# Where the absolute sums over three weight matrices are made: rows of w_sp in z1, wo in the first spatial chunk

## The chip, the core and the metric

The kernel runs on one core of one Trainium2 chip. Five engines, each with its own queue in order, work beside each other: TensorE (PE), VectorE (DVE), ScalarE (ACT), GpSimd (POOL) and SyncE (SP); SP and ACT issue the DMAs. The metric is the device time of one execution in microseconds, the median of several runs.

## What is computed

Two blocks on the same input x (2048 rows, 1024 columns, bf16), mixed by a gate:

```python
x = A_x
g = sigmoid((x * gate_w).sum(-1, keepdims=True))
# A: 32 heads of 32; each row attends to 8 rows, itself and those 2, 4, .. 14 above it
qkv = x @ wqkv; logits = q . k[s - 2w] * 32 ** -0.5; a = (softmax(logits) . v[s - 2w]) @ wo
# B: gMLP
z = gelu(x @ w_in)                       # 3584 columns: z1 the first 1792, z2 the others
z2 = layernorm(z2)                       # over its 1792 columns
gg = einsum('ts,sf->tf', w_sp, z2) + b_sp[:, None]     # w_sp is 2048 x 2048
b = (z1 * gg) @ w_out
return g * a + (1 - g) * b
```

## The kernel before

Nearly all arithmetic is TensorE's, in stages one after the other:

- **z2, first part** (to 37 us of the trace): 128-row tiles of x times 512-column pieces of w_in, gelu on ScalarE (line 308) into the array `z2`.
- **q, k, v** (lines 623 and 643, to 197 us). Rows go to DRAM and come back in another order; the attention itself is VectorE's (lines 349 to 399), eight head groups from here to the end of the spatial chunks, with one exp on ScalarE per group (line 379).
- **z2, second part** (line 303, 198 to 283 us): 14 tiles of 512 columns, then for each of 16 row tiles one of 512 and one of 257 columns (256 and the gate's). ScalarE makes the gelu of each, copies the gate's column (line 312) and, after each pair, sums the squares of the row tile (line 756). VectorE normalizes four row tiles at a time.
- **z1** (line 829, 283 to 380 us): 14 column tiles f, each with four products of 8 matmuls over 512 rows; gelu on ScalarE (line 832) into a slot of `z1s_slots`, from which a DMA stores it to `z1_d` (line 835). The last tiles stay on chip in `z1c_slots` in part.
- **spatial chunks 0 and 1** (`g_chunk`, line 857, 380 to about 482 us): for 512 rows t each, 14 groups of 16 matmuls of z2 by a transposed quarter of w_sp. Each group adds to a PSUM bank that ScalarE has seeded with b_sp (line 787), five groups ahead; ScalarE copies the result out (line 861) and VectorE multiplies it with z1 (line 864).
- **the other 1024 rows** (`seven_products`, line 925): seven products in place of eight, with sums and differences of operands, in fp16 where they are sums. So that they fit, rows of w_sp (and w_out and wo later) are multiplied by powers of two, which are taken from their sums of absolute values.
- **the mix with w_out and wo** (lines 1053 and 1142, to the end).

The sums of absolute values are the subject. Each is one ScalarE instruction over 128 x 2048 elements with an accumulated output, on a block that a DMA has loaded for it:

- *rows of w_sp*, 8 blocks of 128 rows (lines 745 to 748), in z2's second part, with three slots and one junk output in the region EF; they give `row`, from which `row_powers` (lines 799 to 812, VectorE) makes `up` and `down`.
- *w_out* 7 and *wo* 4 blocks (lines 769 to 777), in z1, with two slots in the region CD; they give `w_l1` and `wo_l1`, whose largest values are made powers of two by `whole_power` in three steps.

In chunk 0 the same rows of w_sp are loaded again by DMAs from ScalarE's queue (`natural`, line 872), multiplied by `up` (`scale_rows`: rows 1, 3, 5 on VectorE, line 886; the others on ScalarE, line 890), stored to `wsp_d` (lines 888 and 891) and read back transposed for `seven_products` (line 491, SP). The transposed quarter of w_sp for chunk 1 is loaded by SP at the same time, in four pieces (line 491 too); `scaled_biases` sends the scaled b_sp through DRAM (`bsp_d`, lines 879 and 882), and a pair of attention groups is stored to `o_d` (line 410).

The order is written by hand. A counter of TensorE's columns, `beat`, gives a planned time; `beat.at(t, fn)` puts an instruction into its engine's queue as soon as the matmuls issued so far reach t:

```python
def at(self, t, fn):
    heapq.heappush(self.later, (t, self.n, fn))
def run(self, cols):
    self.now += cols * BEAT          # BEAT = 1 / 2360 us
    self.flush(self.now)
```

VectorE's attention steps are interleaved by an estimate of when VectorE is free. What an engine waits for is set by data and by slots alone, except that every DMA takes one of eight completion counters in turn, over both issuing queues: it isn't issued before the DMA eight places ahead of it has landed.

PSUM has eight banks of 128 x 512 fp32; all stages take theirs from one pool. The names in the profile leave numbers out, so that `z1_d` and `z2_d` are both `z_d`, `w_l1` is `w_l`.

Of the kernel before, what the change touches and what calls it, by code (L numbers as in the profile page):

```python
# [47 lines left out]
CD_OFF = A_OFF + 22016  # L48
EF_OFF = CD_OFF + 19456
# [8 lines left out]
def kernel(  # L58
# [13 lines left out]
    nc = tc.nc  # L72
# [10 lines left out]
    def reg(off, n):  # L83
        return arena[:, off:off + n]
# [32 lines left out]
    row = sm.tile([P, 8], F32, name="row")  # L117
# [6 lines left out]
    w_l1 = sm.tile([P, 7], F32, name="w_l1")  # L124
    v_l1 = s1[:, 0:NF]
    u_l1 = sm.tile([P, NF], F32, name="u_l1")
    top = sm.tile([P, 1], F32, name="top")
# [3 lines left out]
    wo_l1 = sm.tile([P, 4], F32, name="wo_l1")  # L131
# [49 lines left out]
    w1_slots = [reg(EF_OFF + r * 4096, 4096).rearrange("p (k c) -> p k c", k=KT) for r in range(2)]  # L181
    z1s_slots = [reg(EF_OFF + 8192 + r * 2048, 2048).rearrange("p (c t) -> p c t", c=4) for r in range(4)]
    row_slots = [reg(EF_OFF + 10240 + r * 2048, 2048) for r in range(3)]
    row_out = reg(EF_OFF + 8192, 2048)
    wsp_slots = [reg(CD_OFF, 8192).rearrange("p (i a t) -> p i a t", i=16, a=4),
# [10 lines left out]
    nat_slots = [reg(X_OFF + r * S, S) for r in range(8)]  # L196
    look_slots = [reg(CD_OFF + 8192 + r * 2048, 2048) for r in range(2)]
    look_out = reg(CD_OFF + 12288, 2048)
# [32 lines left out]
    wsp_v = B_w_sp.rearrange("(a t) s -> a t s", t=P)  # L231
    wo_v = A_wo.rearrange("(g h d) n -> g h d n", g=NG, h=HG, d=DH)
    sync = nc.sync
# [38 lines left out]
    beat = Beat()  # L272
# [471 lines left out]
    sync.dma_start(b_row[:], bass.AP(tensor=B_b_sp.tensor, offset=B_b_sp.offset + 1024, ap=[[P, 8], [1, P]]))  # L744
    for r in range(8):
        beat.at(beat.now + 1.0 + (1.5 * r if r < 3 else 4.0 * r), lambda r=r: sync.dma_start(row_slots[r % 3], wsp_v[8 + r]))
        beat.at(beat.now + 8.0 + 4.0 * r, lambda r=r: nc.scalar.activation(row_out, row_slots[r % 3], ACT.Abs,  # L747
                                                                           accum_out=row[:, r:r + 1]))
    for i in range(2, 16):
# [17 lines left out]
    wout_v = B_w_out.rearrange("(f p) n -> p f n", p=P)  # L767
    wo_rows = A_wo.rearrange("(k p) n -> p k n", p=P)
    for k in range(11):
        slot = look_slots[k % 2]  # L770
        src = wout_v[:, 2 * k:2 * k + 2, :] if k < 7 else wo_rows[:, 2 * k - 14:2 * k - 12, :]
        total = w_l1[:, k:k + 1] if k < 7 else wo_l1[:, k - 7:k - 6]
        beat.at(beat.now + 2.0 + 7.0 * k, lambda src=src, slot=slot: sync.dma_start(
            slot.rearrange("p (f n) -> p f n", f=2), src))
        beat.at(beat.now + 13.0 + 7.0 * k, lambda total=total, slot=slot: nc.scalar.activation(
            look_out, slot, ACT.Abs, accum_out=total))

    for g in range(NG):
        beat.at(beat.now + 6.0 + 10.0 * g, lambda g=g: turn_wo(g))
    w_steps = whole_power(w_up, omg[:])  # L780
    beat.at(beat.now + 72.0, lambda: (nc.vector.tensor_reduce(top[:], w_l1[:], AX.X, ALU.max), next(w_steps)))

# [30 lines left out]

    beat.at(beat.now + 50.0, row_powers)

    for f in range(NF):
        ch = f // 4
        w1 = w1_slots[ch % 2]
        if f % 4 == 0 and ch in (1, 2):
            load_w1(ch + 1)  # L820
        z1s = z1s_slots[f % 4]
        if f == 4:
# [434 lines left out]
    t0 = beat.now  # L1257
    for r in range(8):
        beat.at(t0 + 6.0 + 3.4 * r, lambda r=r: natural(r))
        beat.at(t0 + 20.0 + 4.0 * r, lambda r=r: scale_rows(r))  # L1260
    for aa in range(4):
        beat.at(t0 + 1.0 + 7.0 * aa, lambda aa=aa: load_wsp(1, aa))
        beat.at(t0 + 50.0 + 2.5 * aa, lambda aa=aa: load_wsp(2, aa))
        beat.at(t0 + 61.0 + 2.5 * aa, lambda aa=aa: load_wsp(3, aa))
# [66 lines left out]
```

## Time and profile before

| | us |
|---|---|
| median of 3 runs | 705.11 (704.88 to 706.19) |
| the profiled execution, its own time | 706.95 |
| its span in the profile | 704.8 |
| TensorE busy | 684.7 |
| VectorE busy | 562.4 |
| ScalarE busy | 416.0 |

The profile gives, for one execution, busy times by engine, the span in 40 slices with the granted TensorE clock and DMA, the chain of work that ended last, and instructions grouped by source line. More views of the trace list who waited for whom, and instructions in order of time: start, duration, engine, line, output and input, and in brackets how long the engine was idle before it and what ended that. In the views of stretches each engine's busy time stands with its instructions in brackets. SPq and ACTq are DMA issues; L747 is line 747.

### The profile page before, as it was taken

How to read it: one execution, taken by the hardware profiler on the slowest of the kernel's cores; microseconds unless marked ns; L12 is line 12 of the kernel's file. 1: busy time of each engine (PE TensorE's matmuls, PEld its weight loads, DVE VectorE, ACT ScalarE, POOL GpSimd, SP SyncE). 2: the span in 40 equal slices, each digit the busy share in tenths (PEclk: the TensorE clock that was granted, in tenths of full speed). 3: DMA queues.
4: the chain of work that ended last, by engine and by line, in shares of the span. 5: the costliest groups of instructions: out<-in, count | busy, mean ns of one | idle time of the engine just before them, and what ended most of it. 6: DMA issues, size and time to landing. Idle time of an engine off the chain costs nothing.

```text
span 704.8 us, 9004 instructions
## 1 busy us (share of the span) xinstructions
PE 684.7 (97%) x3327; PEld 356.2 (51%) x3327; DVE 562.4 (80%) x692; ACT 416.0 (59%) x744; POOL 12.9 (2%) x45
## 2 busy tenths in 40 slices
PE   9999999999996879999999999998999999999997
PEld 4499666666642445444444444443444444444443
DVE  4646999999999278799999985998368789666663
ACT  4368948655553999977866437524986552222232
POOL 0000000000000002200000000000000000000000
PEclk9999999999998999999999999999999999999999
DMA  9995985535498602699978999956411243222220
GB/s 233 187 182 162 208 235 129 153 91 124 133 251 276 268 1 87 164 209 318 340 250 251 295 132 306 263 108 193 134 62 52 81 109 74 60 61 74 61 60 31
DMA packets 189148, 112.87 MB, mean 160 GB/s; under 512 B 146608, under 2 KB 172720, under 8 KB 188848
## 3 DMA queue, kind: packets, MB, share of 16 engines
q1 hardware_dynamic: 187232, 105.48, 56.9%
q10 hardware_dynamic: 1872, 6.82, 3.1%
q8 instruction: 26, 0.43, 0.2%
q14 instruction: 18, 0.15, 0.1%
HBM read 63.71 MB, written 34.41 MB: 139 GB/s over the span
## 4 chain that ended last, share of the span: by engine, by line
PE 86%; ACT 5%; DMA 3%; DVE 2%; SPq 1%; issue 1%; DVEq 0%
PE ps L623 16%; PE ps L829 14%; PE ps L1053 12%; PE ps L925 12%; PE ps L857 10%; PE ps L303 8%; PE ps L643 7%; PE ps L1142 6%; ACT arena L747 2%; DMA arena<-in_B_w_in_dram 2%; ACT arena L308 1%; DMA arena<-in_B_w_sp_dram 1%; PE ps L1132 1%; ACT arena L756 1%; SPq L491 1%
## 5 line engine op out<-in xcount | busy, mean ns | idle before, releaser
L303 PE MATMUL ps<-arena 128*128 128x512 bf16 (+1 forms) x512 | 103.3, 361 | 13.6 <-ACT arena L308 13.0
L623 PE MATMUL ps<-arena 128*128 128x512 bf16 (+1 forms) x640 | 115.8, 337 | 0.0
L857 PE MATMUL ps<-arena 128*128 128x512 bf16 x448 | 97.8, 379 | 0.0
L623 PEld LDWEIGHTS <-arena 128*128 128x128 bf16 x640 | 83.2, 144 | 27.8 <-issue 0.5
L829 PE MATMUL ps<-arena 128*128 128x512 bf16 x448 | 97.0, 379 | 0.0
L1053 PE MATMUL ps<-arena 128*128 128x512 f16 (+1 forms) x392 | 92.8, 379 | 0.0
L925 PE MATMUL ps<-arena 128*128 128x512 bf16 (+1 forms) x392 | 85.7, 379 | 2.2 <-DVE arena L902 2.2
L303 PEld LDWEIGHTS <-arena 128*128 128x128 bf16 x512 | 51.1, 100 | 65.7 <-issue 19.9
L349 DVE TENSOR_TENSOR arena<-arena 128x8192 bf16<-128x8192 bf16 x16 | 70.8, 4422 | 6.8 <-DMA arena<-k_d 6.5
L392 DVE TENSOR_TENSOR arena<-arena,att_A 128x8192 bf16<-128x8192 bf16 x16 | 70.7, 4420 | 1.0 <-DMA arena<-v_d 1.0
L829 PEld LDWEIGHTS <-arena 128*128 128x128 bf16 x448 | 43.8, 98 | 52.6 <-issue 0.2
L857 PEld LDWEIGHTS <-arena 128*128 128x128 bf16 x448 | 43.4, 98 | 52.6 <-issue 0.9
L925 PEld LDWEIGHTS <-arena 128*128 128x128 bf16 (+1 forms) x392 | 37.9, 98 | 48.4 <-DVE arena L902 2.6
L1053 PEld LDWEIGHTS <-arena 128*128 128x128 f16 (+1 forms) x392 | 38.3, 98 | 46.1
L629 ACT CAST arena<-ps 128x512 bf16<-128x512 f32 (+1 forms) x80 | 38.4, 510 | 32.6 <-PE ps L623 32.6
L352 DVE TENSOR_TENSOR arena<-arena 128x4096 bf16<-128x4096 bf16 (+1 forms) x32 | 56.1, 1754 | 0.6
L643 PE MATMUL ps<-arena 128*128 128x512 f16 (+1 forms) x224 | 52.4, 379 | 0.0
L1142 PE MATMUL ps<-arena 128*128 128x512 f16 (+3 forms) x200 | 50.3, 375 | 0.0
L1122 DVE SCALAR_TENSOR_TENSOR arena<-ps,g_s,arena 128x512 bf16<-128x512 f32 (+2 forms) x33 | 24.0, 733 | 28.7 <-ACT arena L1174 20.0
L308 ACT ACTIVATE arena<-ps 128x512 bf16<-128x512 f32 x64 | 34.1, 538 | 19.8 <-PE ps L303 19.8
L832 ACT ACTIVATE arena<-ps 128x512 bf16<-128x512 f32 x56 | 31.5, 599 | 17.0 <-PE ps L829 14.2
L643 PEld LDWEIGHTS <-arena 128*128 128x128 f16 (+1 forms) x224 | 32.2, 144 | 16.1
(203 smaller groups left out, 773.7 us busy)
## 6 DMA issues: line engine op xcount, KB each, us to landing
arena<-k_d SPq DMA_DIRECT2D x8, 960.0 KB, 6.8
arena<-v_d SPq DMA_DIRECT2D x8, 960.0 KB, 5.6
arena<-in_A_wqkv_dram SPq DMA_DIRECT2D x24, 256.0 KB, 4.9
z_d<-arena SPq DMA_DIRECT2D x12, 512.0 KB, 6.8
arena<-q_d SPq DMA_DIRECT2D x8, 512.0 KB, 6.4
o_d<-arena SPq DMA_DIRECT2D x4, 1024.0 KB, 13.2
arena<-in_B_w_in_dram SPq DMA_DIRECT2D x4, 1024.0 KB
arena<-in_B_w_sp_dram SPq DMA_DIRECT2D x8, 512.0 KB, 5.3
```

The source lines that it names most:

```text
L303: nc.tensor.matmul(ps[:, 0:N], xT[:, kt, i * P:(i + 1) * P], w2[c][:, kt, 0:N], start=(kt == 0), stop=(kt == KT - 1))
L308: nc.scalar.activation(z2[:, 4 * c:4 * c + n // P, i, :], ps[:, 0:n].rearrange("p (f q) -> p f q", q=P), ACT.Gelu_apprx_tanh, accum_out=s1 ...
L349: TT(prod.rearrange("p (w j c) -> p w j c", w=W, j=8, c=C), in0, in1, ALU.mult)
L352: return lambda: TT(pv[:, :, 0:half], pv[:, :, 0:half], pv[:, :, half:2 * half], ALU.add)
L392: TT(prod.rearrange("p (w j d h) -> p w j d h", w=W, j=8, d=DH, h=HG), in0, in1, ALU.mult)
L623: nc.tensor.matmul(ps[:, n0:n1].rearrange("p (t c) -> p t c", c=C), lhsT, wgt[:, pos0:pos1, kt, :], start=(kt == 0), stop=(kt == KT - 1))
L643: nc.tensor.matmul(dst[:].rearrange("p (t c) -> p t c", c=C), lhs(k), rhs[:, :, k, :], start=first and k == 0, stop=k == 3, skip_group_che ...
L829: nc.tensor.matmul(ps[:], w1[:, kt, (f % 4) * P:(f % 4 + 1) * P], xT[:, kt, 512 * c:512 * (c + 1)], start=(kt == 0), stop=(kt == KT - 1))
L857: nc.tensor.matmul(ps[:], z2[:, f, i, :], wsp[:, i, :, :].rearrange("p a t -> p (a t)"), start=False, stop=(i == 15), skip_group_check=True)
L925: nc.tensor.matmul(dst[:], lhs[:, k, :], rhs(k), start=False, stop=k == 7, skip_group_check=True)
L1053: nc.tensor.matmul(dst[:], lhs[:, j, :], rhs(j), start=first and j == 0, stop=j == 6, skip_group_check=not first)
L1142: nc.tensor.matmul(dst, lhs[:, k, :], rhs[:, k, :], start=first and k == 0, stop=k == 3, skip_group_check=not first)
```

## The change

The eight loads and sums of w_sp's rows leave z2's second part. In z1 one sequence of fifteen loads and sums stands, alternating between w_sp (8) and w_out (7): a load every 5.2 us of planned time, its sum due 9.5 us after the load. They have three places instead of two; the third is the fourth slot of `z1s_slots`, which has three left. `row_powers` is due 89 us into z1 instead of 50, the first step of w_out's power 87 instead of 72. The four loads and sums over wo go into chunk 0, due 3, 7, 11 and 15 us after its start, with their sums 9.5 us later, in three places of the region EF; their junk output is the last slot of the natural rows.

```diff
-    z1s_slots = [... for r in range(4)]
-    row_slots = [reg(EF_OFF + 10240 + r * 2048, 2048) for r in range(3)]
-    row_out = reg(EF_OFF + 8192, 2048)
+    z1s_slots = [... for r in range(3)]
...
-    look_slots = [reg(CD_OFF + 8192 + r * 2048, 2048) for r in range(2)]
+    look_slots = [reg(off, 2048) for off in (CD_OFF + 8192, CD_OFF + 10240, EF_OFF + 14336)]
...
-    for r in range(8):
-        beat.at(beat.now + 1.0 + (1.5 * r if r < 3 else 4.0 * r), lambda r=r: sync.dma_start(row_slots[r % 3], wsp_v[8 + r]))
-        beat.at(beat.now + 8.0 + 4.0 * r, lambda r=r: nc.scalar.activation(row_out, row_slots[r % 3], ACT.Abs,
-                                                                           accum_out=row[:, r:r + 1]))
...
-    for k in range(11):
-        slot = look_slots[k % 2]
-        src = wout_v[:, 2 * k:2 * k + 2, :] if k < 7 else wo_rows[:, 2 * k - 14:2 * k - 12, :]
-        total = w_l1[:, k:k + 1] if k < 7 else wo_l1[:, k - 7:k - 6]
-        beat.at(beat.now + 2.0 + 7.0 * k, lambda src=src, slot=slot: sync.dma_start(
-            slot.rearrange("p (f n) -> p f n", f=2), src))
-        beat.at(beat.now + 13.0 + 7.0 * k, lambda total=total, slot=slot: nc.scalar.activation(
-            look_out, slot, ACT.Abs, accum_out=total))
+    def look(t, src, slot, out, total):
+        beat.at(t, lambda: sync.dma_start(slot.rearrange("p (a n) -> p a n", a=src.shape[1]) if len(src.shape) == 3 else slot, src))
+        beat.at(t + 9.5, lambda: nc.scalar.activation(out, slot, ACT.Abs, accum_out=total))
+
+    for k in range(15):
+        if k % 2:
+            src, total = wout_v[:, k - 1:k + 1, :], w_l1[:, k // 2:k // 2 + 1]
+        else:
+            src, total = wsp_v[8 + k // 2], row[:, k // 2:k // 2 + 1]
+        look(beat.now + 2.0 + 5.2 * k, src, look_slots[k % 3], look_out, total)
...
-    beat.at(beat.now + 72.0, lambda: (nc.vector.tensor_reduce(top[:], w_l1[:], AX.X, ALU.max), next(w_steps)))
+    beat.at(beat.now + 87.0, lambda: (nc.vector.tensor_reduce(top[:], w_l1[:], AX.X, ALU.max), next(w_steps)))
...
-    beat.at(beat.now + 50.0, row_powers)
+    beat.at(beat.now + 89.0, row_powers)
...
-        z1s = z1s_slots[f % 4]
+        z1s = z1s_slots[f % 3]
...
+    for k in range(4):
+        look(t0 + 3.0 + 4.0 * k, wo_rows[:, 2 * k:2 * k + 2, :], reg(EF_OFF + 8192 + 2048 * (k % 3), 2048),
+             nat_slots[7], wo_l1[:, k:k + 1])
```

No instruction of TensorE or GpSimd is added, removed or moved in its queue; VectorE's are the same in number.

More of the change, by code (lines that the diff above doesn't have):

```diff
@@ L181 @@
     w1_slots = [reg(EF_OFF + r * 4096, 4096).rearrange("p (k c) -> p k c", k=KT) for r in range(2)]
-    z1s_slots = [reg(EF_OFF + 8192 + r * 2048, 2048).rearrange("p (c t) -> p c t", c=4) for r in range(4)]
-    row_slots = [reg(EF_OFF + 10240 + r * 2048, 2048) for r in range(3)]
-    row_out = reg(EF_OFF + 8192, 2048)
+    z1s_slots = [reg(EF_OFF + 8192 + r * 2048, 2048).rearrange("p (c t) -> p c t", c=4) for r in range(3)]
     wsp_slots = [reg(CD_OFF, 8192).rearrange("p (i a t) -> p i a t", i=16, a=4),
```

## The prediction

> **What bounds the kernel now.** I read the page first, then the waits inside the stage from which the change takes work, then that stage engine by engine.
>
> ```profile
> span 704.8 us, 9004 instructions
> PE 684.7 (97%) x3327; PEld 356.2 (51%) x3327; DVE 562.4 (80%) x692; ACT 416.0 (59%) x744; POOL 12.9 (2%) x45
> PE   9999999999996879999999999998999999999997
> PEclk9999999999998999999999999999999999999999
> ```
>
> TensorE bounds the kernel: the slices are full except in two places, around 220 to 265 us and around 485 us. Only there can an edit that removes no matmul gain. The waits between 196 and 285 us (who waited for whom; total, times, longest):
>
> ```profile
> ACT arena L747 <- DMA arena<-in_B_w_sp_dram: 15.6, 1, 15.6
> PE ps L303 <- ACT arena L308: 13.0, 5, 6.4
> DVE att_m L370 <- ACT att_L L379: 13.8, 1, 13.8
> ```
>
> L747 is the sum over a row block of w_sp, which the change takes out of this stage; L303 are the z2 matmuls, L308 their gelus. ScalarE is in order, so its wait of 15.6 us for the first row block holds back every gelu behind it, TensorE runs out of PSUM banks, and the attention's exp (L379), further down the same queue, keeps VectorE idle for 13.8 us. The timelines of TensorE and ScalarE there:
>
> ```profile
> 197.64 22.61 PE L303 MATMUL ps<-arena 128*128 128x512 bf16 x104
> 226.64 16.92 PE L303 MATMUL ps<-arena 128*128 128x512 bf16 x88 [6.39 <-ACT arena L308]
> 246.66 4.41 PE L303 MATMUL ps<-arena 128*128 128x512 bf16 x16 [3.11 <-ACT arena L308]
> 263.44 19.36 PE L303 MATMUL ps<-arena 128*128 128x512 bf16 x112 [1.29 <-ACT arena L308]
> 282.79 2.53 PE L829 MATMUL ps<-arena 128*128 128x512 bf16 x11
> ```
>
> ```profile
> 223.40 1.91 ACT L747 ACTIVATE arena<-arena 128x2048 bf16<-128x2048 bf16 x1 [15.63 <-DMA arena<-in_B_w_sp_dram]
> 241.01 1.28 ACT L379 ACT_TABLE_LOAD   x1
> 242.30 0.63 ACT L379 ACTIVATE att_L<-att_L 128x512 f32<-128x512 f32 x1
> 279.31 0.58 ACT L308 ACTIVATE arena<-ps 128x512 bf16<-128x512 f32 x1
> 282.07 0.58 ACT L308 ACTIVATE arena<-ps 128x512 bf16<-128x512 f32 x1
> ```
>
> and two stretches with TensorE's granted clock (third number from the end; the last two are DMA share and GB/s):
>
> ```profile
> 226.64:230.00 3.36, 3.36 (x8) 1.13 (x8) 1.88 (x2) 3.36 (x7) 0.00 (x0) 0.50 0.76 296
> 246.66:251.00 4.34, 4.34 (x16) 2.14 (x16) 4.31 (x2) 4.34 (x8) 0.00 (x0) 0.61 0.02 4
> ```
>
> After each of the two long stalls TensorE runs at about half clock, so the stall costs more than its idle time.
>
> **Part 1: the eight row sums leave z2.** The first 104 matmuls ran unhindered: 22.61 us for 13 tiles, 1.739 us a tile of 512 columns; the 257-column tile is taken as 257/512 of it, 0.873. The stage has 14 tiles of the first kind, then 16 pairs of both: 30 x 1.739 + 16 x 0.873 = 66.1 us. It took 282.79 - 197.64 = 85.15. So 19.0 us are to be had: the idle time, the half-clock time, and matmuls that ran at ScalarE's pace.
>
> Does ScalarE allow it? Its cadence at the end of the stage is one pair in 282.07 - 279.31 = 2.76 us against 2.61 on TensorE. Without the sums it reaches the first pair at about 223.7 (197.64 + 15 x 1.739) and needs 16 x 2.76 + 3.2 (the exp and the table loads on both sides of it, 2 x 1.28 + 0.63) = 47.4 us, to 271.1. TensorE would be done at 263.8. The lag of 7.3 us is 5.6 tiles at 1.3 us; there are eight banks, so about two tiles, 2.5 us, remain. The exp itself must not wait for VectorE:
>
> ```profile
> 219.22 0.69 DVE L376 TENSOR_TENSOR att_L<-att_L,att_m 128x512 f32<-128x512 f32 x1
> 242.97 0.42 DVE L370 TENSOR_TENSOR att_m<-att_L 128x256 f32<-128x256 f32 x1 [13.85 <-ACT att_L L379]
> ```
>
> Its input is ready at 219.9, and ScalarE gets there at about 225. VectorE then loses its 13.85 us wait and most of its small waits on the gelus, so it moves up by about as much as TensorE. On SyncE's queue eight loads (4 MB) go, four of which waited for a slot; the attention loads behind them go out earlier. Part 1: **-19.0 us**.
>
> **Part 2: fifteen looks in z1.** Before, eleven sums ran there at the cadence of 7 us; now fifteen at 5.2, with three slots, one of which was the fourth z1 output slot.
>
> ```profile
> 282.80:379.85 97.05, 97.05 (x451) 43.93 (x450) 91.18 (x88) 74.73 (x132) 4.85 (x10) 1.00 0.85 256
> 371.74 1.09 ACT L832 ACTIVATE arena<-ps 128x512 bf16<-128x512 f32 x2 [2.69 <-DMA z_d<-arena]
> SPq L835 <- ACT arena L832: 20.3, 5, 6.5
> z_d<-arena SPq DMA_DIRECT2D x12, 512.0 KB, 6.8
> ```
>
> ScalarE goes from 74.7 to 82.3 of 97 us (four more at 1.91), DMA from 256 GB/s by 2 MB in 97 us to 278. A z1 slot is now reused after two tiles of f, 2 x 6.93 = 13.9 us, where it had 20.8; a store takes 3.0 (its due time) + up to 6.5 (SyncE's wait) + 6.8 (landing) = 16.3 at worst, so some gelus wait by up to 2.4 us. With eight banks TensorE has some 12 us in hand once ScalarE has caught up: cost **0**, and if that cover is gone 2.4 us a time. The row powers and the first step of w_out's power move 39 and 15 us later on VectorE; nobody asks for them before the next stage: the row powers, due at 282.8 + 89 = 371.8, are first used by the biases' transpose on TensorE (due 8 us into that stage, 387.9) and by the row scaling at 401.76 (below).
>
> **Part 3: four wo sums in the first spatial chunk.** This is the doubtful part. The chunk starts at 379.85 in the old trace; times here are the old trace's, everything being moved up alike. Rows of SyncE's queue, ScalarE and VectorE:
>
> ```profile
> 391.37 2.65 SPq L491 DMA_TRANSPOSE arena<-in_B_w_sp_dram  x1
> 394.75 0.63 SPq L410 DMA_DIRECT2D o_d<-arena  x1
> 395.43 15.06 SPq L491 DMA_TRANSPOSE arena<-in_B_w_sp_dram  x1
> 410.58 0.53 SPq L882 DMA_DIRECT2D arena<-bsp_d  x1
> arena<-bsp_d SPq DMA_DIRECT2D x1, 256.0 KB, 15.4
> ```
>
> ```profile
> 394.12 0.59 ACT L861 CAST arena<-ps 128x512 bf16<-128x512 f32 x1 [2.58 <-PE ps L857]
> 401.76 2.01 ACT L890 ACTIVATE arena<-arena,up 128x2048 bf16<-128x2048 bf16 x1
> 411.64 0.59 ACT L861 CAST arena<-ps 128x512 bf16<-128x512 f32 x1 [0.25 <-PE ps L857]
> 426.04 0.35 ACTq L891 DMA_DIRECT2D wsp_d<-arena  x1
> 428.58 0.58 ACT L787 CAST ps<-arena 128x512 f32<-128x512 bf16 x1
> 429.70 0.43 DVE L864 TENSOR_TENSOR arena<-arena 128x512 bf16<-128x512 bf16 x1 [8.12 <-ACT arena L861]
> ```
>
> and from the chain of work and the busy times by stretch (engines PE, PEld, DVE, ACT, POOL; clock, DMA share, GB/s):
>
> ```profile
> 415.37 34.71 PE ps L857 x160
> 400.00:425.00 25.00, 25.00 (x116) 11.14 (x115) 20.18 (x24) 9.72 (x15) 0.38 (x4) 1.00 1.14 207
> ```
>
> The last of four transposed loads of w_sp (395.43) sits 15.06 us in SyncE's queue, behind the store of o_d. ScalarE's store of row block 2 (L891, 426.04) waits on a completion counter that it shares with the load of bsp_d (410.58 + 15.4 = 425.96). ScalarE stands meanwhile; TensorE lives on five seeded groups. A group is 16 matmuls, 34.71 / 10 = 3.47 us. When one's result is copied at 411.64, five seeded groups are left: dry at 411.64 + 5 x 3.47 = 429.0, just when the next seed is written (428.58 to 429.16). There is no slack.
>
> In the new program order that store shares its counter with the last transposed load, which is ahead of bsp_d: the wait ends at or before 425.96. Against that, the fourth wo load waits for the first wo sum, which stands behind the copy at 394.12 and ends at about 394.65 + 1.9 = 396.6; the transposed load of 391.37 goes out 0.5 after it, 5.7 later than before, and the o_d store and the last transposed load with it. Four sums add 7.6 us to a ScalarE that was busy 9.72 us of the 25 from 400. The row load before the last now waits for the o_d store. So the wait moves by between 425.96 + 5.7 at one end and, if the load lands at once when SyncE lets it go (410.5 + 5.7 = 416.2), -9.8 at the other. I take the middle, some 2 us earlier: no stall of TensorE, and VectorE's 8.12 us wait shrinks by about as much.
>
> The second hole of the page:
>
> ```profile
> PE ps L925 <- DVE arena L902: 2.2, 1, 2.2
> ```
>
> L902 is VectorE's third table for the next stage, at the end of an unbroken row of work since 429.70. What VectorE gains or loses there passes to this wait: between -2.2 and +5.7 by the bounds above. I take -1.1.
>
> **Sum.** 19.0 + 0 + 1.1 = 20.1 us. The profiled execution took 706.95 us (span 704.8, 2.15 around it), so 686.85; the median of the runs shown, 705.11, is 1.84 below it: **685.0 us**.
>
> **The rivals.**
> *The last transposed load is pushed out (B).* The full 5.7 us with the old landing time: seed ready at 429.16 + 5.7, TensorE dry for up to 6 us. For: 2 MB are put in front of it, in a stretch that ran at 1.14 of its DMA share. Against: bsp_d is out of the wait. A 3.11 us stall already left the clock at 0.61, so up to 1.7 us more. Worst 20.1 - 6 - 1.7 = 12.4 won, 692.7; middle 689.
> By the Trainium skill, "DMA: Bandwidth & Descriptors", section "Issuing engines are not separate DMA queues", loads issued by SyncE and by ScalarE share the same 16 DMA engines; by that rule the wo loads also delay the row loads on ScalarE's queue, which speaks for B. The share over 1 agrees.
> The Trainium skill, "TensorE: Matmul & The Clock Gate", section "What's actually happening", puts the clock at half after an idle window of about 3.4 us until a busy window has passed; the rows with 0.50 and 0.61 agree, and by it a stall under 3 us would cost only itself.
> *ScalarE paces z2 still (C).* If the banks don't cover the 7.3 us lag, z1 starts when ScalarE lets it: 16 x 0.15 + 3.2 = 5.6 us lost, 690.6. For: 2.5 us of cover is thin. Against: nothing else in this stage holds banks.
> *Three z1 slots bind (D).* With one or two late stores, 2.4 us each past the cover, 687 to 690. The same mechanism ends slower than before if the stores pace z1: each of 11 reuses must lose 1.96 us to eat 21.5 us, that is a store must take 13.9 + 3 x 1.96 = 19.8 us every time, against 16.3 at worst now. Then 706.5 or more.
> *The change doesn't empty z2.* Only if another wait stands at the head of ScalarE's queue; the exp is the candidate, and its input is ready 5 us ahead. It is part of C.
>
> **How the numbers follow.** Forecast 0.62 (from 683.9, the second hole gone too, to 686.5); B 0.20, of which 0.01 slower by a stall past its bound; C 0.09; D 0.09, of which 0.03 slower and 0.01 no change. The range from 683.0, 0.9 under the sum without any hole, to 691.5 leaves out the worst of B and the strong D. Faster by over 0.2% (1.4 us, about what these runs can tell from no change) 0.95, within it 0.01, slower 0.04.
>
> **What would show it.** Right: no wait of L303 on L308 over 1 us, clock 1.00 throughout from 197 us on, z1's first matmul at 263 to 265, VectorE's wait on the exp gone; the chunk starting at about 361; no idle TensorE in it. B shows as a wait of L857 near 410 (new time) on ScalarE's seeds or on the transposed load; C as gaps of L303 on L308 late in z2 or of L829 in its first tiles; D as gelus of z1 waiting for z_d stores, with TensorE waiting on them. The forecast is wrong if z1 starts after 267, or if the second hole is over 4 us.

## The result, and the profile after

The median went from 705.11 to 696.53 us (694.99 to 698.5); the ratio is 0.9877 (0.9846 to 0.9907). The forecast, 685.0 with 683.0 to 691.5, was too low. The same program, run again beside the experiments, took 687.70 (685.43 to 691.75) and 686.82 (685.98 to 694.73). So its 16 executions reach from 685.4 to 698.5, where the kernel before stayed between 704.3 and 707.0; why they spread is most of what follows. The first four all lie at 695 or above; of the later twelve, run on two chips, only two come near that (694.6 and 694.7). On each of those two chips the times spread too, so the execution has a part in it; whether the chip has one as well is not shown. The first profile is of an execution of 698.5 us, the longest.

The page of it: span, busy times, TensorE in slices and its granted clock.

```profile
span 696.4 us, 8966 instructions
...
PE 679.1 (98%) x3276; PEld 355.4 (51%) x3327; DVE 561.7 (81%) x692; ACT 416.4 (60%) x744; POOL 12.9 (2%) x45
...
PE   8999999999999999999999989978999999999997
...
PEclk9999999999999999999999999998999999999999
```

The hole around 220 to 265 us is gone from both rows. The one around 470 us is deeper than it was, and it has a forerunner at 410. TensorE's timeline, and z1 as one stretch (engines PE, PEld, DVE, ACT, POOL; clock, DMA share, GB/s):

```profile
197.99 66.33 PE L301 MATMUL ps<-arena 128*128 128x512 bf16 x360
264.16 26.06 PE L825 MATMUL ps<-arena 128*128 128x512 bf16 x118
...
361.07 10.52 PE L853 MATMUL ps<-arena 128*128 128x512 bf16 x47
...
407.68 3.61 PE L853 MATMUL ps<-arena 128*128 128x512 bf16 x16 [0.46 <-ACT ps L783]
413.23 20.88 PE L853 MATMUL ps<-arena 128*128 128x512 bf16 x94 [1.94 <-ACT ps L783]
...
466.03 1.89 PE L921 MATMUL ps<-arena 128*128 128x512 f16 x8 [1.89 <-ACT ps L783]
472.68 27.56 PE L921 MATMUL ps<-arena 128*128 128x512 f16 x111 [4.76 <-DVE arena L898]
```

```profile
264.16:361.07 96.91, 96.44 (x443) 43.83 (x450) 91.57 (x92) 79.72 (x135) 3.43 (x10) 1.00 0.91 273
```

(Lines above 184 have moved up by two to four: L301, L825, L853, L921, L898, L860 and L390 here are L303, L829, L857, L925, L902, L864 and L392 before.) z2's second part is one unbroken row of 66.33 us, z1 too, and chunk 0 starts at 361.07 where it started at 379.85. So 18.8 us are won there. The span is only 8.4 us shorter: some 10 were given back after 361 us. Who waited for whom from there to 475 us (total, times, longest):

```profile
DVE arena L860 <- ACT arena L857: 13.4, 2, 8.2
...
ACT ps L783 <- DMA arena<-in_B_w_sp_dram: 7.2, 1, 7.2
ACT arena L412 <- DMA o_d<-arena: 6.3, 1, 6.3
DVE arena L390 <- DMA arena<-v_d: 5.6, 1, 5.6
...
PE ps L921 <- DVE arena L898: 4.8, 1, 4.8
...
PE ps L853 <- ACT ps L783: 2.4, 2, 1.9
...
PE ps L921 <- ACT ps L783: 1.9, 1, 1.9
```

ScalarE stands twice, 7.2 us until a row load has landed and 6.3 us until the o_d store has. VectorE waits 13.4 us for the groups that ScalarE should have copied, and 5.6 us for an attention load (L390). Before, the same two were, between the same times:

```profile
DVE arena L864 <- ACT arena L861: 9.2, 2, 8.1
DVE arena L392 <- DMA arena<-v_d: 1.0, 1, 1.0
```

TensorE then stands 2.4 us on seeds in the chunks, 1.9 us on the first seeds of the seven products, and 4.8 us on VectorE's third table: 9.1 us. The queues of SP and ScalarE, the page's row of the o_d store, and three stretches show what stood behind that:

```profile
378.43 4.01 SPq L489 DMA_TRANSPOSE arena<-in_B_w_sp_dram  x1
...
383.82 22.02 SPq L489 DMA_TRANSPOSE arena<-in_B_w_sp_dram  x1
```

```profile
395.40 0.34 ACTq L868 DMA_DIRECT2D arena<-in_B_w_sp_dram  x1
406.04 0.33 ACTq L868 DMA_DIRECT2D arena<-in_B_w_sp_dram  x1
```

```profile
o_d<-arena SPq DMA_DIRECT2D x4, 1024.0 KB, 22.9
```

```profile
382.00:394.00 12.00, 11.95 (x56) 5.45 (x56) 9.70 (x7) 5.49 (x6) 0.00 (x0) 1.00 1.17 87
...
472.68:477.00 4.32, 4.32 (x11) 1.57 (x12) 3.08 (x3) 0.69 (x2) 0.00 (x0) 0.50 0.95 247
477.00:480.00 3.00, 3.00 (x12) 1.21 (x11) 0.14 (x1) 1.66 (x4) 0.00 (x0) 0.74 1.06 392
```

From 382 to 394 us the DMA engines are busy at a share of 1.17 and move 87 GB/s, with the third transposed load of w_sp, two row loads, the attention's v_d load, the o_d store and a row store on the way. (Of wo hardly anything is: its last load has landed at 383.3.) I call this the clogged stretch. Row load 5 (395.40) has to wait until row load 3, eight places ahead of it over both queues, has landed (395.38); row load 6 (406.04) waits for the o_d store, which takes 22.9 us. Both stand in ScalarE's queue ahead of copies and seeds. After the stall at 472.68 the clock is 0.50 up to 477 and 0.74 on average from there to 480, so it is halved for some 5.9 us; that adds about 3 us to the 9.1. Less the 2.2 us that TensorE stood at the same place before, this is 9.9 of the 10.4 us given back.

### The profile page after: what moved, and what is told of

Same layout as the page of the kernel before. It is cut to its first block, busy times and chain, and to the rows that moved or that the text cites. A ratio compares the mean times of both kernels' runs of the same rounds, so it can differ in the third digit from the quotient of the medians.

```text
span 696.4 us, 8966 instructions
## 1 busy us (share of the span) xinstructions
PE 679.1 (98%) x3276; PEld 355.4 (51%) x3327; DVE 561.7 (81%) x692; ACT 416.4 (60%) x744; POOL 12.9 (2%) x45
## 4 chain that ended last, share of the span: by engine, by line
PE 85%; DMA 5%; SPq 4%; DVE 3%; ACT 1%; issue 1%; ACTq 0%; DVEq 0%
PE ps L621 16%; PE ps L825 14%; PE ps L301 13%; PE ps L921 12%; PE ps L1049 12%; PE ps L641 7%; PE ps L1138 6%; PE ps L853 4%; SPq L489 3%; DMA o_d<-arena 3%; PE ps L1128 1%; DMA arena<-wsp_d 1%; DMA arena<-in_B_w_in_dram 1%; DVE arena L350 0%; DVE arena L894 0%
## 5 line engine op out<-in xcount | busy, mean ns | idle before, releaser
L621 PE MATMUL ps<-arena 128*128 128x512 bf16 (+1 forms) x637 | 115.6, 337 | 0.2
L853 PE MATMUL ps<-arena 128*128 128x512 bf16 x439 | 97.6, 379 | 2.9 <-ACT ps L783 2.4
L301 PE MATMUL ps<-arena 128*128 128x512 bf16 (+1 forms) x501 | 97.3, 352 | 1.6 <-DMA arena<-in_B_w_in_dram 1.1
L825 PE MATMUL ps<-arena 128*128 128x512 bf16 x439 | 96.6, 379 | 0.5
L921 PE MATMUL ps<-arena 128*128 128x512 f16 (+1 forms) x385 | 88.1, 388 | 7.2 <-DVE arena L898 4.8
L1049 PE MATMUL ps<-arena 128*128 128x512 f16 (+1 forms) x380 | 91.2, 379 | 0.5
L390 DVE TENSOR_TENSOR arena<-arena,att_A 128x8192 bf16<-128x8192 bf16 x16 | 70.7, 4419 | 5.6 <-DMA arena<-v_d 5.6
L301 PEld LDWEIGHTS <-arena 128*128 128x128 bf16 x512 | 50.1, 98 | 48.6 <-issue 1.0
L853 PEld LDWEIGHTS <-arena 128*128 128x128 bf16 x448 | 43.4, 98 | 55.3 <-issue 3.6
L825 PEld LDWEIGHTS <-arena 128*128 128x128 bf16 x448 | 43.7, 98 | 52.4
L921 PEld LDWEIGHTS <-arena 128*128 128x128 bf16 (+1 forms) x392 | 38.6, 100 | 55.3 <-issue 6.4
L641 PE MATMUL ps<-arena 128*128 128x512 f16 (+1 forms) x224 | 52.4, 379 | 0.0
L306 ACT ACTIVATE arena<-ps 128x512 bf16<-128x512 f32 x64 | 34.2, 536 | 28.7 <-PE ps L301 28.6
L765 ACT ACTIVATE arena<-arena 128x2048 bf16<-128x2048 bf16 x19 | 36.3, 1910 | 6.5 <-DMA arena<-in_B_w_out_dram 4.4
## 6 DMA issues: line engine op xcount, KB each, us to landing
o_d<-arena SPq DMA_DIRECT2D x4, 1024.0 KB, 22.9
```

The source lines that it names most:

```text
L301: nc.tensor.matmul(ps[:, 0:N], xT[:, kt, i * P:(i + 1) * P], w2[c][:, kt, 0:N], start=(kt == 0), stop=(kt == KT - 1))
L390: TT(prod.rearrange("p (w j d h) -> p w j d h", w=W, j=8, d=DH, h=HG), in0, in1, ALU.mult)
L621: nc.tensor.matmul(ps[:, n0:n1].rearrange("p (t c) -> p t c", c=C), lhsT, wgt[:, pos0:pos1, kt, :], start=(kt == 0), stop=(kt == KT - 1))
L641: nc.tensor.matmul(dst[:].rearrange("p (t c) -> p t c", c=C), lhs(k), rhs[:, :, k, :], start=first and k == 0, stop=k == 3, skip_group_che ...
L825: nc.tensor.matmul(ps[:], w1[:, kt, (f % 4) * P:(f % 4 + 1) * P], xT[:, kt, 512 * c:512 * (c + 1)], start=(kt == 0), stop=(kt == KT - 1))
L853: nc.tensor.matmul(ps[:], z2[:, f, i, :], wsp[:, i, :, :].rearrange("p a t -> p (a t)"), start=False, stop=(i == 15), skip_group_check=True)
```

## The experiments

**Which part of the wo looks costs it.** Four theories: the 2 MB of wo loads clog chunk 0 (bytes); four more DMAs turn the completion counters (counters); the fourth wo load, which has no place until the first sum is done, holds SP's queue (queue); four sums are too much for ScalarE. Four kernels tell them apart. The first has no wo look in chunk 0:

```diff
-    for k in range(15):
-        if k % 2:
+    for k in range(19):
+        if k > 14:
+            src, total = wo_rows[:, 2 * k - 30:2 * k - 28, :], wo_l1[:, k - 15:k - 14]
+        elif k % 2:
...
-        look(beat.now + 2.0 + 5.2 * k, src, look_slots[k % 3], look_out, total)
+        look(beat.now + 2.0 + 4.2 * k, src, look_slots[k % 3], look_out, total)
```

> The sums over wo go back to z1, at the end of the one sequence there (19 loads every 4.2 us in place of 15 every 5.2); none is left in the first spatial chunk. If the 10 us that the change lost after z1 all come from the wo looks in chunk 0, by whatever means, z2 stays as in the changed kernel (z1 starts at 264), the second hole is back at about 2 us, and the time is 684 to 687. If the loss comes from elsewhere (the order in which the rows' sums now end, or the attention moved up), the holes after the chunks stay and the time is 694 to 697. If 19 looks are too many for z1's three slots, TensorE waits in z1 for the gelus there and the chunk starts later than 361.

It took 688.75 us (688.27 to 689.69). The holes after chunk 0 are gone; z1 pays. The waits of its end, 340 to 366 us:

```profile
ACT arena L765 <- DMA arena<-in_A_wo_dram: 3.9, 3, 2.2
...
PE ps L827 <- ACT arena L830: 2.7, 2, 1.7
```

The sums (L765) wait for their blocks, gelus behind them come late, TensorE stands 2.7 us. So the 10 us were lost in chunk 0, and 19 looks are too many for z1. The others edit the four looks of chunk 0:

```diff
 # loads left out
+        beat.at(t0 + 12.5 + 4.0 * k, lambda k=k: nc.scalar.activation(
+            nat_slots[7], reg(EF_OFF + 8192 + 2048 * (k % 3), 2048), ACT.Abs, accum_out=wo_l1[:, k:k + 1]))
 # sums left out
+    nc.gpsimd.memset(wo_l1[:], 64.0)
+        beat.at(t0 + 3.0 + 4.0 * k, lambda k=k: sync.dma_start(..., wo_rows[:, 2 * k:2 * k + 2, :]))
 # loads cut to 64 columns, sums as they were
+        beat.at(t0 + 3.0 + 4.0 * k, lambda k=k, slot=slot: sync.dma_start(slot[:, 0:64], wo_rows[:, 2 * k, 0:64]))
```

> The four loads of wo in chunk 0 are left out; their four sums stay at the same planned times on ScalarE and read what stands in the three places (the power over wo is thus of other data). Theories: bytes (2 MB of loads slow the other transfers of chunk 0): 685 to 688. Counters (four more DMAs turn the eight completion counters so that ScalarE's row loads come to wait for slow DMAs): 685 to 688. Queue (the fourth wo load waits for the first sum and holds SP's transposed load, the o_d store and the last transposed load behind it): 685 to 688. ScalarE (four sums of 1.9 us are too much for it in chunk 0): stays at 694 to 697.

> The four loads of wo in chunk 0 stay; the four sums are left out (their results are set to a constant early on), so the fourth load has no sum to wait for. Theories: bytes: stays at 694 to 697. Counters: stays at 694 to 697. Queue: 685 to 688, with the third transposed load of w_sp some 3 to 5 us earlier on SP. ScalarE: 685 to 688.

> The four loads of wo in chunk 0 are cut to 64 of 2048 columns (16 KB each in place of 512 KB), the sums stay as they are; the counters turn as in the changed kernel, and the fourth load still waits for the first sum. The power over wo is of other data. Theories: bytes: 685 to 688. Counters: stays at 694 to 697, with row load natural(5) waiting for natural(3) and natural(6) for the o_d store on ScalarE's queue. Queue: stays at 694 to 697. ScalarE: stays at 694 to 697.

Without loads 685.55 (685.05 to 686.31), without sums 686.1 (685.83 to 696.17, three of four below 686.2), with tiny loads 685.82 (685.62 to 686.32). ScalarE's theory falls, since the sums alone cost nothing; and the counters alone are not enough: with tiny loads row load 6 waits for the o_d store as it does in the changed kernel, but the store has landed by 395.9 us. (That is no proof that the counters have no part; more on this below.) That the loads alone run three times at 686 and once at 696.17 was foreseen by none. The 696.17 us execution was not profiled, so it is not shown that it lost its time in the same way.

**Is it the fourth load's wait, or chance?** Four places in place of three, and the changed kernel once more:

```diff
-        look(t0 + 3.0 + 4.0 * k, ..., reg(EF_OFF + 8192 + 2048 * (k % 3), 2048),
+        look(t0 + 3.0 + 4.0 * k, ..., reg(EF_OFF + 8192 + 2048 * k, 2048),
```

> The changed kernel with four places for the wo loads of chunk 0 in place of three (the fourth is z1's third look slot), so that the fourth load no longer waits for the first sum; loads, sums, bytes and counters stay. Queue theory (that one wait sets SP's transposed loads, the v_d load and the o_d store into the bad time): 685 to 688, with the third transposed load landing by about 388 as in the kernel without sums. If each of the four ingredients only adds a little and it takes all together (the loads' bytes and the sums): 694 to 697, with the transposed load's 256-byte packets again at 70 ns or more.

> The changed kernel once more, for how often it loses the 10 us. If the slow stretch of DMA in chunk 0 (382 to 394 us) is set by the kernel's order, every execution is at 694 to 699. If it is a matter of chance at the edge of some timing, a part of them is at 685 to 688.

Four places: 686.01 (685.67 to 686.19). The changed kernel: 688.24, 685.67, 688.96, 691.75, 685.43 and 687.17. It is the execution that differs, not the program. The profiled one (688.24), same window and groups as above:

```profile
DVE arena L860 <- ACT arena L857: 10.9, 2, 8.0
...
PE ps L921 <- DVE arena L898: 1.8, 1, 1.8
...
DVE arena L390 <- DMA arena<-v_d: 0.6, 1, 0.6
```

Of the same order of instructions VectorE lost 11.5 us here and 19.0 in the first profile; TensorE lost 1.8 and 9.1. The first profile's longer attention wait (5.6 against 0.6) comes from a second clogged stretch: its second transposed load of scaled rows took 12 us from issue to landing (424.8 to 436.8) and this one's 7.3, and the v_d load behind it on SP went out at 436.4 against 429.1.

The fourth place of that kernel was one in which two z1 tiles of the second chunk stand, which it overwrites; with the slot of row block 6 in its stead:

```diff
+        look(t0 + 3.0 + 4.0 * k, ..., nat_slots[6] if k == 3 else reg(EF_OFF + 8192 + 2048 * k, 2048),
```

> The changed kernel with a fourth place for the fourth wo load (the slot of row block 6, free until 26 us into the chunk; in the earlier kernel with four places that place held z1 tiles 12 and 13 of the second chunk, which it overwrote). Loads, sums and bytes as in the changed kernel; the fourth load no longer waits for the first sum. If that wait is what opens the way to the slow stretch: 685 to 687 in nearly all of six executions. If the slow stretch is open to every order with the wo loads in it: 1 to 3 of six above 688.

686.39 (685.9 to 686.59), over four executions. Its stretch from 382 to 394 us, and two of its waits:

```profile
382.00:394.00 12.00, 12.00 (x58) 5.43 (x56) 11.90 (x12) 9.24 (x14) 0.00 (x0) 1.00 1.09 339
```

```profile
DVE arena L860 <- ACT arena L857: 4.4, 1, 4.4
DVE arena L390 <- DMA arena<-v_d: 3.5, 1, 3.5
```

339 GB/s at nearly the same share, where the first profile has 87. All 2 MB of wo were loaded in both, and the last load has landed by 382.8 here and 383.3 there: wo's bytes come ahead of the stretch and are hardly in it.

**Is it row loads that overlap a transposed load?** Row loads 4 to 7 held back by 4 us; and, without wo loads, all eight closer together:

```diff
+        beat.at(t0 + 6.0 + 3.4 * r + (4.0 if r > 3 else 0.0), lambda r=r: natural(r))   # first kernel
+        beat.at(t0 + 6.0 + 2.0 * r, lambda r=r: natural(r))                             # second, no wo loads
```

> The changed kernel a third time, beside the next three. If what it loses is a lottery inside each execution, its times spread from 685.4 up to 698 as they did over the first two; if it belongs to the chip, all of them lie together, near 687 or near 697.

> The changed kernel with the loads of row blocks 4 to 7 on ScalarE's queue due 4 us later; nothing else moves. Overlap theory (a transposed load goes slow where it starts while two or more of ScalarE's 512 KB transfers are in flight: the third one in the changed kernel, at 382, beside row loads 3 and 4): the third transposed load lands by 388, and the time is 685 to 688 with little spread. Bytes theory (the 4 MB on the way in chunk 0 are too many, whoever starts when): the third transposed load still takes until 393 to 396 and the time stays spread over 685 to 698. If row blocks 4 to 7 are simply needed earlier: slower, 690 and more, with ScalarE waiting for the row loads at their scaling.

> The changed kernel without the wo loads (the four sums stay, over what stands in the places, as in the first kernel without loads, which took 685.55), and with the eight row loads 2.0 us apart instead of 3.4. Overlap theory: with more of ScalarE's transfers in flight when the transposed loads start, the slow stretch comes back without any wo byte: 256-byte packets at 60 ns or more for 5 us or longer, 687 to 697. Bytes theory: there is no more traffic than in the kernel without loads, and the rows are there earlier: 685 to 686.

The changed kernel again: 694.63, 686.15, 687.35, 686.28, 694.73, 685.98. Rows held: 688.22 (685.33 to 693.26), as widely spread as without. Its profile is of the 685.33 us execution, without a clogged stretch before 396 us, so what the long executions did there is not seen. Rows close: 688.24 (687.01 to 688.86), but by another road. From 384 to 392 us its DMAs move 302 GB/s and more. The load of row block 7 comes to wait for the o_d store, and in this kernel the junk output of the last two sums falls on row block 7 after its load, so that a sum stands until that has landed, 13.1 us. The times that the overlap theory gave for rows held did not come, and rows close shows that more overlap does not bring the stretch back. Waits of 361 to 475 us, first the 694.63 us execution of the changed kernel, then rows close:

```profile
DVE arena L860 <- ACT arena L857: 13.6, 2, 8.1
...
PE ps L921 <- DVE arena L898: 3.2, 1, 3.2
...
PE ps L853 <- ACT ps L783: 2.6, 2, 1.9
...
DVE arena L390 <- DMA arena<-v_d: 2.0, 1, 2.0
```

```profile
ACT arena L1258 <- DMA arena<-in_B_w_sp_dram: 13.1, 1, 13.1
DVE arena L860 <- ACT arena L857: 12.5, 2, 12.1
...
PE ps L853 <- ACT ps L783: 1.6, 2, 1.1
PE ps L921 <- DVE arena L898: 1.2, 1, 1.2
```

**What the changed places are worth alone, and other places for wo.** The kernel before with wo alone moved to chunk 0; the kernel before with the row sums still in z2 but 16 us later (the loads too, from the fourth on); and the wo looks in the seven products (two places in the region A, sums written in place, the steps of the powers moved):

```diff
+    for k in range(7):             # z1, the kernel before; the four wo looks stand in chunk 0 as in the change
...
-        beat.at(beat.now + 8.0 + 4.0 * r, lambda r=r: nc.scalar.activation(row_out, ...
+        beat.at(beat.now + 24.0 + 4.0 * r, lambda r=r: nc.scalar.activation(row_out, ...
...
+        if (n, place) in ((1, 2), (1, 4), (2, 2), (2, 4)):      # seven products
+            nc.scalar.activation(wo_places[k % 2], wo_places[k % 2], ACT.Abs, accum_out=wo_l1[:, k:k + 1])
```

> The kernel before, with its four wo sums alone moved to chunk 0 as in the change; the rows of w_sp stay in z2. If the wo move costs its 10 us by itself, in any surrounding: 712 to 716. If the cost comes only with chunk 0 moved up against the attention, or takes the place of a loss that the kernel before already has in the same stretch (its own slow stretch of DMA from 406 to 422): 703 to 707.

> The kernel before, with the sums over w_sp's rows still in z2 but due 16 us later (and the fourth and later loads with them), so that the first sum finds its block loaded. It leaves nothing out. If the 19 us of z2 were the wait for the first load alone: z1 starts at 265 to 268 and the time is 687 to 691. If the sums' own 15 us on ScalarE count too (ScalarE 271 without them, 286 with them, less some 10 us that eight banks and z1's first tiles cover): z1 starts at 272 to 277 and the time is 694 to 700.

> The four wo loads and sums leave chunk 0 for the first three of the seven products, where the DMA engines are busy for 0.2 to 0.3 of the time: two places at the end of the region A, the sums written in place, the steps of wo's power in product 4 and 5 in place of chunk 0 and 1, those of the power before them one place later. The rows stay in z1. If the loss is only what chunk 0 does to the DMAs: 685 to 686, with no execution above 688. If the sums get into ScalarE's copies between the products, or the power's steps make TensorE wait: 687 to 690, with waits of the seven products on ScalarE or on VectorE.

The wo move alone: 706.43 (704.7 to 714.42, three of seven above 711), so the spread comes with it in the old surroundings too. Rows later: 698.3 (698.0 to 698.9). Its waits in z2 and z1's first row:

```profile
PE ps L303 <- ACT arena L308: 8.1, 6, 1.7
...
ACT arena L747 <- DMA arena<-in_B_w_sp_dram: 1.3, 1, 1.3
```

```profile
277.16 23.04 PE L829 MATMUL ps<-arena 128*128 128x512 bf16 x106
```

The wait for the first block is down from 15.6 to 1.3, yet z1 starts at 277.16, only 5.6 earlier: the sums' work on ScalarE is most of what z2 lost. In the seven products: 694.17 (693.22 to 695.42), steady and bad. There the four sums hold up copies that the next product needs (waits from 455 to 510 us), and after the wait of 3.1 us the clock is 0.50 for 5.7 us:

```profile
PE ps L921 <- ACT ps L944: 4.1, 2, 3.1
```

**A version that beats both.** Two wo looks at the end of z1's sequence, two in chunk 0:

```diff
+    for k in range(17):            # z1, k > 14: wo
+        look(beat.now + 2.0 + 4.7 * k, src, look_slots[k % 3], look_out, total)
...
+    for k in range(2, 4):          # chunk 0
+        look(t0 + 3.0 + 4.0 * (k - 2), wo_rows[:, 2 * k:2 * k + 2, :], ...
```

> Two of the four wo sums back to the end of z1's sequence (17 looks every 4.7 us), two stay in chunk 0, 3 and 7 us into it. If half the bytes in chunk 0 leave the way to the slow stretch shut and z1 bears 17: 685 to 687 in all executions. If z1's end is full already (as with 19, which cost 3): 687 to 688, steady. If the slow stretch needs only one wo load in the wrong place: spread up to 695.

> The changed kernel without the loads of wo (sums over what stands in the places), once more, for how steady it is. If the slow stretch needs the wo loads: all six executions at 685 to 687. If it comes without them too: one or more above 688.

Split: 685.91 (685.61 to 686.82), a ratio of 0.9726 (0.9713 to 0.9739) to the kernel before. No loads, again: 685.77 (685.32 to 686.36). In the kernels with no wo loads or tiny ones, 13 executions of 13 lie from 685.05 to 686.36.

**How the clogged stretch reaches the end.** First the rows made late on purpose, then ScalarE and VectorE given work of no use; all three on the kernel without wo loads:

```diff
+        beat.at(t0 + 6.0 + 3.4 * r + (6.0 if r > 3 else 0.0), lambda r=r: natural(r))                  # rows late
+        beat.at(t0 + 20.0 + 4.0 * r + (9.0 if r > 1 else 0.0), lambda r=r: scale_rows(r))
...
+    for t, many in ((27.0, 7), (39.0, 6)):                                                             # ScalarE stands
+        beat.at(t0 + t, lambda many=many: [nc.scalar.activation(abs_wide, abs_wide, ACT.Abs) for _ in range(many)])
...
+    beat.at(t0 + 24.0, lambda: [TT(abs_wide, abs_wide, abs_wide, ALU.max) for _ in range(14)])         # VectorE late
```

> The kernel without wo loads, with the row blocks made late on purpose: loads of blocks 4 to 7 due 6 us later, scalings of blocks 2 to 7 (and so their stores) due 9 us later, which is how late they were in the first profile of the changed kernel (the store of block 2 at 410 instead of 401). No slow stretch of the first kind is made. If lateness of the scaled rows is the link by which the slow stretch costs 10 us (the transposed loads of the scaled rows queue ahead of the attention's next load on SP, VectorE waits for that, is late with its table, and TensorE stands at the start of the seven products): 690 to 697, with TensorE waiting for VectorE there by 3 us or more. If the rows have that slack and the slow stretch costs its time in another way: 685 to 687.

> The kernel without wo loads, in which ScalarE is kept from its queue twice in chunk 0 by work of its own that nobody needs (seven instructions over 128 x 1024 elements, about 7.4 us, from 27 us into the chunk, and six, 6.4 us, from 39 us), about as long and where it stood in the first profile of the changed kernel (7.2 us to 395.4 and 6.3 us to 406.0). No DMA is added or moved. If ScalarE's standing is the link (its copies of the groups come late, VectorE waits for them, and the seeds run out): VectorE waits 11 to 14 us in the chunks, TensorE stands some 2.5 us on seeds and 2 to 4 us on VectorE's table, 690 to 695. If the DMAs themselves are the link (the attention's loads): no hole, 685 to 688.

> The kernel without wo loads, with 14 additional VectorE instructions over 128 x 1024 elements (about 10 us in all) from 24 us into chunk 0, on data that nobody needs; ScalarE and the DMAs have the same work. If what reaches the end is VectorE's lost time alone, whatever lost it (7.9 us of waits in the chunks cost nothing, 11.5 cost 1.8 us, 15.6 cost 3.2 and 19.0 cost 4.8 at the first of the seven products): 10 us beside the 4.5 that this kernel waits already make a hole of 2 to 5 us there, 688 to 692. If it takes ScalarE's standing as well: 685.5 to 687.

Rows late: 685.75 (684.99 to 686.14), with the last row store issued at 424.0 against 425.9 in the first profile; that lateness alone costs nothing. ScalarE standing: 687.57 (687.41 to 687.73) where 690 to 695 were expected, and TensorE does not stand on seeds. VectorE late: 687.04 (686.93 to 687.26), under the 688 to 692 expected; the hole is there, but of 1.5 us instead of 2 to 5. The two in order, VectorE's additional work from its timeline:

```profile
DVE arena L860 <- ACT arena L857: 11.2, 2, 7.8
...
PE ps L921 <- DVE arena L898: 1.3, 1, 1.3
```

```profile
388.69 10.13 DVE L1260 TENSOR_TENSOR arena<-arena 128x1024 bf16<-128x1024 bf16 x14
```

```profile
PE ps L921 <- DVE arena L898: 1.5, 1, 1.5
...
DVE arena L390 <- DMA arena<-v_d: 1.1, 1, 1.1
```

Seven profiles of the changed order together, in us: what VectorE lost in the two chunks (waits L860 and L390, and the useless work), less what TensorE itself lost there on seeds, and the wait for the third table.

| profile | VectorE lost | TensorE lost before the table | difference | table wait |
|---|---|---|---|---|
| four places, valid | 7.9 | 0 | 7.9 | 0 |
| ScalarE stands | 11.2 | 0 | 11.2 | 1.3 |
| VectorE late | 11.2 | 0 | 11.2 | 1.5 |
| changed, 688.24 | 11.5 | 0 | 11.5 | 1.8 |
| rows close | 12.5 | 1.6 | 10.9 | 1.2 |
| changed, 694.63 | 15.6 | 2.6 | 13.0 | 3.2 |
| changed, 698.5 | 19.0 | 4.3 | 14.7 | 4.8 |

The table wait is the difference less 9.7 to 9.9 in every row that has one. So VectorE has some 9.8 us to lose in the chunks of this order, whoever takes them, and each further one goes to TensorE. The other profiles of kernels with the rows in z1 lose 2.0 to 6.1 us there and have no wait on the table, as this says. The kernel before does not lie on this line: it loses 10.2 us and waits 2.2.

This settles the link from VectorE's lost time to the end. It does not settle what sets off the clogged stretch in one execution and not in the next. Wo's bytes don't make it by themselves. The profile of before has one, later in chunk 0:

```profile
406.00:422.00 16.00, 16.00 (x74) 7.03 (x73) 14.25 (x20) 5.63 (x10) 0.38 (x4) 1.00 1.20 113
```

And the kernel without wo loads has one, beside its fourth transposed load, in an execution of 685.58 us. Its stretch, and row loads 5 and 6 in it:

```profile
386.00:394.00 8.00, 7.95 (x38) 3.62 (x38) 7.93 (x9) 7.43 (x15) 0.00 (x0) 1.00 1.26 127
```

```profile
385.98 0.33 ACTq L868 DMA_DIRECT2D arena<-in_B_w_sp_dram  x1
392.56 0.33 ACTq L868 DMA_DIRECT2D arena<-in_B_w_sp_dram  x1
```

There the stretch costs nothing. With four DMAs fewer, row loads 5 and 6 have their counters from older transfers that are down already (row load 6 from row load 3, landed at 384.8), and ScalarE first stands at a DMA at 397, for 4.5 us at a store. In the changed kernel the same two loads fall on transfers that lie in the stretch. So, as I read these traces, the loss takes both: a clogged stretch, and DMAs of ScalarE's queue that wait for what lies in it. With tiny loads the waits are short because the stretch is missing; without loads it is there, and the waits are missing. No kernel here turns the counters alone while the stretch is present, so that reading is not tested by itself.

With the fourth load free of its wait the 10 us were not seen in the eight executions of the two kernels with four places. The kernel without sums has that wait removed too, and one of its four took 696.17; so it isn't shown that this wait opens the way. The split and the second kernel with four places ran on a chip for which no execution of the changed kernel is on record, so their steadiness rests on four executions each. The times of the kernel before do not spread; with four wo looks and three places in chunk 0 they do, in both surroundings, and without wo's bytes there (13 executions, on two chips) they do not.

## Why the prediction was wrong

- **Part 1, right to half a microsecond.** 66.1 and z1 at 263.8 were forecast, 66.33 and 264.16 came, the chunk at 361.07, no wait of L301. The kernel with later sums shows that removing ScalarE's work counted and not just the first wait: it won 5.6 of the 19.
- **Part 2, right.** 15 looks cost nothing: ACT was put at 82.3 of 97 us and DMA at 278 GB/s, the row of z1 has 79.72 and 273, and TensorE does not stand. So C and D did not happen. With 19 looks z1 does pay, 2.7 us, but not in D's way: no gelu waits for a z_d store there; the sums wait for their blocks.
- **Part 3 is the step that failed.** "I take the middle, some 2 us earlier: no stall of TensorE, and VectorE's 8.12 us wait shrinks by about as much." The bounds of that step knew one wait of ScalarE, on row block 2's store. In the changed order there are two others: row load 5 on row load 3, which was not seen, and row load 6 on the o_d store, which was written down ("the row load before the last now waits for the o_d store") and given no price. The delay on SP's queue was right: the third transposed load goes out at 378.43, 5.8 us later than before when the 18.78 us by which chunk 0 moved are added. But the step let the transfers behind it take as long as before, and in the clogged stretch they don't: the o_d store lands at 406.01, by the same count about 14 us later than before, against about 6 in four places, valid. VectorE's waits on ScalarE's copies and on attention loads, 9.2 and 1.0 us before (the 8.12 is the longest of them), became 13.4 and 5.6 in the first profile and 10.9 and 0.6 in the second, where some 2 us less were forecast.
- **The second hole** was put at 2.2 - 1.1, bounds -2.2 and +5.7. In the first profile the wait on the table is 4.8, so 2.6 more than before; with 4.3 on seeds and some 3 for the half clock it makes up 9.9 of the 10.4 us. In the second profile it is 1.8. "Or if the second hole is over 4 us" was the sign to look for, and it came.
- **B** had the seeds, at up to 6 us (2.4 came in the chunks), and by its worst, 692.7, missed the way over VectorE, which costs as much again. Its rule from the Trainium skill ("DMA: Bandwidth & Descriptors", section "Issuing engines are not separate DMA queues"), that DMAs issued by either engine run on the same 16 DMA engines, fits the clogged stretch, in which transfers of SP and ScalarE are slow together; but 339 GB/s with the same loads show that shared engines alone don't give the price. The Trainium skill, "TensorE: Matmul & The Clock Gate", section "What's actually happening", has the clock at half after an idle window of about 3.4 us. These rows agree at both ends: after 4.76 us idle the clock is 0.50, after 1.47 us (VectorE late) it stays at 1.00. In between somewhat less than 3.4 us was enough here: 3.11 us before, and 3.1 us in the kernel with the looks in the seven products.
- **The range** treated chunk 0 as one case with one time. The same program spreads over 13 us there; five of its 16 executions lie within 1.3 us of the forecast (685.43 to 686.28), and the median of the first four does not. That the medians of the two later groups, 687.70 and 686.82, lie inside the range is luck of the execution: the step left this loss out, and they hold it in part.
- The rest of the sum stands: with chunk 0 relieved the time is 685.5 to 686.4, against 685.0.

## What to carry to other kernels

Before a load goes into a stage in which the DMA engines are full, list for each DMA of a computing engine's queue the transfer that it must wait for, and price every one by that transfer's longest landing: an in-order engine that stands at a DMA issue stops its copies too. Then ask how much the next engine can lose before the bound one notices (here 9.8 us): in this case below it the delay is free, above it each microsecond counts, and a kernel that sits at that edge spreads from one execution to the next. A few repeats tell more there than one careful profile.

## What was not expected of the hardware

- The DMA engines can be busy throughout and move a quarter of what they move in another execution: 87 GB/s at a share of 1.17 (first profile) and 339 at 1.09 (four places, valid) over the same 12 us, with much the same transfers on the way. In the clogged stretch the transposed load's 256-byte packets take 70 to 106 ns on average by the trace instead of 18 to 20, ScalarE's 4096-byte packets 330 to 830 instead of 159. It comes without any wo load too (127 GB/s at 1.26), where it cost nothing.
- A transposed load holds SP's queue until the store issued ahead of it is nearly down: 22.02 us at 383.82, to 405.84, where the o_d store landed at 406.01, and 18.89 us in the second profile, to 403.43 with the store landing at 403.64. In the other profiles too the issue of the fourth transposed load ends 0.1 to 1.7 us before that store has landed.
